# Linear attention, then a squared-ReLU MLP: q of the first batch in two halves, KV copy on VectorE, weight and v loads reordered, block sums later

## The chip, the cores and the metric

One core of one Trainium2 chip. The metric is the device time of one execution in microseconds (us). A time below is a median of the stated number of executions. The experiments ran on three chips (12, 13 and 14 in the record); each ratio is taken against executions of before from the same rounds.

## The reference

```python
# q, k, v: (8 batches, 8 heads, 576 tokens, 64); phi(x) = [relu(x)*cos, relu(x)*sin] by position
q_p, k_p = phi(q), phi(k)
kv  = einsum('bhsf,bhsd->bhfd', k_p, v);  z = sum_s(k_p)
x   = einsum('bhsf,bhfd->bhsd', q_p, kv) / (einsum('bhsf,bhf->bhs', q_p, z) + 1e-6)
h   = x.reshape(4608, 512) @ w_in          # w_in 512 x 2048
out = (relu(h)**2) @ w_out                 # w_out 2048 x 512
```

## The kernel before

Each batch has 512 tokens as four tiles of 128 and a tail of 64. TensorE works through a fixed list of "slots": for batch 0, slots 0 to 7 are eight steps of the hidden layer (`gemm1`) and 8 to 15 the output layer (`gemm2`); batch 1 has slots 16 to 25 and 26 to 33. Steps 0 to 3 take tiles 0 and 1 through the four blocks of w_in (512 columns each), steps 4 to 7 tiles 2 and 3. Pieces of the next batches' attention hang on slots. The order on every engine is the order of the program. From batch 1 on, part of the output layer uses sums and differences of w_out's blocks (`w2_sum`), so that fewer products are needed.

```python
def load(src, nm, b, eng):                       # q, k or v of one batch
    main = inp.tile([P, H, J, D], F32, name=nm, tag=nm, bufs=2)
    tail = inp.tile([P, HH, D], F32, name=nm + "t", tag=nm + "t", bufs=2)
    eng.dma_start(out=main[:, :, :, :],
                  in_=src[b, :, 0:MAIN, :].rearrange("h (p j) d -> p h j d", j=J))
    ...                                          # two DMAs for the tail

def att_kv(b, part):
    ...                                          # KV and z of all heads, in PSUM
    if part == 1:
        nc.scalar.copy(out=kvzs[b].rearrange("p (a h) e -> p a (h e)", a=2),
                       in_=kz[:, :, 0 : HH * E1])

def gemm1(b, s):
    ...
    step = P if b == 0 and s % 4 == 0 else w     # 128 columns at a time, or 256
    for c in range(0, w, step):
        for i in range(nh):
            for kb in range(KB):
                nc.tensor.matmul(out=hps[:, i, c:c+step], lhsT=w1sb[:, kb, hb*P:(hb+1)*P], ...)
    nc.scalar.activation(out=rt, in_=hps, func=ACTF.Relu)   # the square, on VectorE, follows

# the start
load_batch(0, nc.sync, "kvq")
constants(); warm(34)                            # matmuls of zeros
...                                              # features of k, casts of v
att_v(0, J - 1, nc.gpsimd, H - 1, H)             # a small GpSimd cast: it waits for v,
for i in range(4): load_w1(i, 4)                 # and so w_in's loads start behind v
load_batch(1, nc.gpsimd, "q")
load_w2(0, 4)
load_batch(1, nc.gpsimd, "kv")
for i in range(1, 4): load_w2(i, 4)
load_batch(2, nc.gpsimd, "qkv")
att_kv(0, 0); att_kv(0, 1)
warm(8)
att_feat(0, 0); att_feat(0, 1)
...                                              # transposes, numerator, division, transposes
for s in range(len(slots)): run(s)
```

## Time and profile before

| what | before |
|---|---|
| time | 290.11 us, median of 3 (289.47 to 290.32) |
| span in the profile | 288.9 us, and that execution took 290.67 us |
| TensorE busy, clock granted | 97%, 1.00 |
| first hidden-layer matmul | 19.18 us |
| GpSimd's DMA queue idle before q's tail of batch 2 | 11.34 us, to 47.53 us |
| first numerator of batch 2 | 79.32 us, with a wait |

The span is the time from the first to the last instruction in the profile; the time adds some 1.8 us. But for a few short holes before 100 us, TensorE is full from the first hidden-layer matmul to its last one, which ends at 285.5 us. The change leaves the last 3.4 us, without matmuls, as they are, so a microsecond is won only before 19 us or in a hole (a stretch in which TensorE waits).

### The profile page before, as it was taken

What the parts mean: (1) busy time and instruction counts of PE and PEld (TensorE: products, weight loads), DVE (VectorE), ACT (ScalarE), POOL (GpSimd) and SP (SyncE); (2) the same over time, 40 slices, a digit from 0 to 9 for tenths busy, and PEclk for the clock granted to TensorE, in tenths of its full rate; (3) what the DMA queues carried; (4) which work ended last, traced back from release to release, by engine and by line L of the source; (5) the groups of instructions that cost most, each with busy time, mean ns of one, the idle gap of its engine ahead of it and who ended that gap; (6) DMA issues with size and microseconds to landing.
All of it is one profiled execution on the core that took longest, in us unless ns stands there. A gap on an engine that the chain in (4) does not pass through costs nothing.

```text
span 288.9 us, 7286 instructions
## 1 busy us (share of the span) xinstructions
PE 281.2 (97%) x3038; PEld 236.0 (82%) x3045; DVE 202.0 (70%) x452; ACT 163.8 (57%) x249; POOL 39.1 (14%) x67
## 2 busy tenths in 40 slices
PE   8989999999899999999999999999999999999995
PEld 3569855788568888898988888888998988889884
DVE  1367765597399399877598777977677877547485
ACT  3476653579758759555783358835695551155210
POOL 1462604660000000100002000000000000000002
PEclk9999999999999999999999999999999999999999
DMA  7999995999988899899519985399808530200015
GB/s 209 298 203 283 355 210 182 317 355 278 121 150 199 151 295 208 207 284 255 167 75 205 336 181 166 93 248 310 220 16 204 144 49 2 122 26 0 2 73 148
DMA packets 76785, 53.04 MB, mean 184 GB/s; under 512 B 52016, under 2 KB 71984, under 8 KB 76752
## 3 DMA queue, kind: packets, MB, share of 16 engines
q1 hardware_dynamic: 66960, 29.24, 46.4%
q0 software_dynamic: 9648, 23.20, 27.6%
q8 instruction: 24, 0.39, 0.6%
q10 hardware_dynamic: 144, 0.13, 0.1%
q14 instruction: 9, 0.07, 0.1%
HBM read 36.70 MB, written 9.44 MB: 160 GB/s over the span
## 4 chain that ended last, share of the span: by engine, by line
PE 84%; DMA 8%; DVE 3%; SPq 2%; ACT 1%; issue 1%; ACTq 0%
PE hps L383 40%; PE ya L525 9%; PE yc L525 9%; PE yu L525 7%; DMA qpT<-qp 5%; PE yv L525 5%; PE num L310 3%; DMA q<-in_q_dram 3%; PE yps L432 2%; PE kz L241 2%; PE yh L432 2%; PE tq L284 1%; SPq L69 1%; PE yps L456 1%; DVE ysb L537 1%
## 5 line engine op out<-in xcount | busy, mean ns | idle before, releaser
L383 PEld LDWEIGHTS <-w1sb 128*128 128x128 bf16 x1312 | 112.9, 98 | 12.7 <-issue 2.0
L383 PE MATMUL hps<-xT,w1sb 128*128 128x256 bf16 (+1 forms) x1056 | 119.1, 269 | 0.7 <-ACT rt L391 0.2
L391 ACT ACTIVATE rt<-hps 128x1024 bf16<-128x1024 f32 x72 | 73.7, 1024 | 66.1 <-PE hps L383 43.7
L398 DVE TENSOR_TENSOR gT<-rt 128x1024 bf16<-128x1024 bf16 x64 | 43.9, 686 | 20.9 <-ACT rt L391 20.9
L525 PEld LDWEIGHTS <-gs 128*128 128x128 bf16 x480 | 46.8, 98 | 5.4
L525 PEld LDWEIGHTS <-gT 128*128 128x128 bf16 x312 | 29.8, 98 | 3.5
L410 POOL DMA_DIRECT2D out_dram<-ysb x14 | 7.6, 542 | 170.8 <-DVE ysb L537 144.9
L181 ACT ACTIVATE kp<-k,sin_col 128x512 bf16<-128x512 f32 x32 | 22.4, 717 | 3.0 <-DMA k<-in_k_dram 3.0
L324 DVE TENSOR_TENSOR x<-num,rden 128x512 bf16<-128x512 f32 x32 | 22.1, 691 | 1.1
L181 ACT ACTIVATE qp<-q,sin_col 128x512 bf16<-128x512 f32 x32 | 22.1, 722 | 0.8 <-DMA q<-in_q_dram 0.7
L320 DVE TENSOR_SCALAR den<-num 128x8 f32<-128x8 f32 (+1 forms) x40 | 6.5, 163 | 21.7 <-PE num L310 21.6
L521 DVE TENSOR_TENSOR gs<-gT 128x1024 bf16<-128x1024 bf16 x26 | 17.8, 684 | 0.0
L171 DVE TENSOR_SCALAR qp<-q,cos_col 128x512 bf16<-128x512 f32 x32 | 15.1, 497 | 1.7 <-DMA q<-in_q_dram 1.7
L525 PE MATMUL ya<-w2t,gs 128*128 128x256 bf16 x120 | 15.6, 273 | 0.0
L525 PE MATMUL yc<-w2sb,gs 128*128 128x256 bf16 x120 | 15.6, 273 | 0.0
L525 PE MATMUL yu<-w2t,gs 128*128 128x256 bf16 x120 | 15.6, 273 | 0.0
L383 PE MATMUL hps<-xTt,w1sb 128*128 128x128 bf16 x256 | 15.1, 219 | 0.2 <-ACT rt L391 0.2
L200 ACT CAST vext<-v 128x512 bf16<-128x512 f32 x23 | 14.1, 614 | 1.8 <-DMA v<-in_v_dram 1.8
L525 PE MATMUL yu<-w2sb,gs 128*128 128x256 bf16 x112 | 14.5, 273 | 0.0
L576 ACT COPY s<-yu 128x256 f32<-128x256 f32 x14 | 5.2, 373 | 15.6 <-PE yu L525 15.6
L525 PE MATMUL yc<-w2sb,gT 128*128 128x256 bf16 x104 | 13.5, 273 | 0.0
L525 PE MATMUL yv<-w2t,gT 128*128 128x256 bf16 x104 | 13.5, 273 | 0.0
(97 smaller groups left out, 333.5 us busy)
## 6 DMA issues: line engine op xcount, KB each, us to landing
out_dram<-ysb POOLq DMA_DIRECT2D x14, 512.0 KB, 4.5
k<-in_k_dram SPq DMA_DIRECT2D x5, 1024.0 KB, 7.5
v<-in_v_dram SPq DMA_DIRECT2D x5, 1024.0 KB, 8.2
q<-in_q_dram SPq DMA_DIRECT2D x5, 1024.0 KB, 6.1
q<-in_q_dram POOLq DMA_DIRECT2D x3, 1024.0 KB, 12.5
k<-in_k_dram POOLq DMA_DIRECT2D x3, 1024.0 KB, 9.0
v<-in_v_dram POOLq DMA_DIRECT2D x3, 1024.0 KB, 8.9
w1sb<-in_moe_w_in_dram POOLq DMA_DIRECT2D x4, 512.0 KB, 8.7
```

Of the source, the lines that this page charges most:

```text
L171: nc.vector.tensor_scalar(out=dst[:, :, 0:D], in0=src, scalar1=0.0, scalar2=cos_col[:, j : j + 1], op0=ALU.max, op1=ALU.mult,)
L181: nc.scalar.activation(out=dst[:, :, D:F], in_=src, func=ACTF.Relu, scale=sin_col[:, j : j + 1])
L200: copy(out=vx[:, j, h0:h1, 0:D], in_=piece("v", b, j)[:, h0:h1, :])
L310: nc.tensor.matmul(out=out, lhsT=lhsT, rhs=kvz[:, half * HH + hh, :], start=True, stop=True)
L324: nc.vector.tensor_tensor(out=x_of(b, j).rearrange("p (b k) (l d) -> p b k l d", b=n, l=2), in0=n4[:, :, :, 0:D].rearrange("p b (k l) d -> ...
L383: nc.tensor.matmul(out=out, lhsT=w1sb[:, kb, hb * P : (hb + 1) * P], rhs=rhs, start=(kb == 0), stop=(kb == KB - 1),)
L391: nc.scalar.activation(out=rt[:, :, :], in_=hps[:, :, :], func=ACTF.Relu)
L398: nc.vector.tensor_tensor(out=dst, in0=rt[:, :, :], in1=rt[:, :, :], op=ALU.mult)
L410: eng.dma_start(out=dst, in_=y.rearrange("p i c -> p (i c)") if n > 1 else y[:, c0:c1])
L432: nc.tensor.matmul(out=ypss[b][tt], lhsT=gTs[b][:, hb, tt * P : (tt + 1) * P], rhs=w2sb[:, hb, :], start=(hb == 0), stop=(hb == HB - 1),)
L521: nc.vector.tensor_tensor(out=t[:, :, :], in0=in0, in1=in1, op=op)
L525: nc.tensor.matmul(out=acc, lhsT=lhs[:, hb, :], rhs=rhs[:, hb, :], start=(hb == 0), stop=(hb == HB2 - 1),)
```

## The change

Intent: let the first two tiles of batch 0 start when half of q has landed; keep the KV copy out of ScalarE's way; let w_out's second block arrive before TensorE needs it; shift batch 1's attention by a slot as its v then lands later; take the block sums off VectorE where it was full.

```diff
-    def load(src, nm, b, eng):
+    def load(src, nm, b, eng, parts=1):
...
+        for i in range(parts):
+            js = slice(i * J // parts, (i + 1) * J // parts)
+            eng.dma_start(
+                out=main[:, :, js, :],
+                in_=src[b, :, 0:MAIN, :].rearrange("h (p j) d -> p h j d", j=J)[:, :, js, :],
+            )
...
-        if part == 1:
-            nc.scalar.copy(...)
+        if part == 1 and b:
+            att_kvz(b, nc.scalar.copy)
+
+    def att_kvz(b, copy):
+        copy(out=kvzs[b]..., in_=kzs[b][:, :, 0 : HH * E1])
...
-        step = P if b == 0 and s % 4 == 0 else w
+        step = P if b < 2 and s in (0, 4) else w
...
-    at(18, att_d, 0, J)
-    at(19, att_x_pe, 0, J, True)
+    at(19, att_d, 0, J)
+    at(20, att_x_pe, 0, J, True)
     plan(
         1,
         k=(8, 8, 8, 9, 9),
         f=(4, 5, 6, 12, 13),
-        kv=(10, 10),
-        d=(11, 13, 15, 17, 19),
-        t=(5, 6, 7, 16, 17),
-        x=(12, 14, 16, 18, 20),
+        v=(10, 10, 10, 10, 10),
+        kv=(11, 11),
+        d=(12, 14, 16, 17, 20),
+        t=(5, 6, 7, 16, 19),
+        x=(13, 15, 17, 18, 21),       # and the odd tiles' and the tail's copies go to VectorE
...
-    for n, s in ((1, 12), (2, 15)):
-        at(s, w2_sum, n)
-    for n, s, c in ((4, 18, 0), (4, 19, 1), (3, 30, 0), (3, 31, 1)):
-        late.setdefault(s, []).append((w2_sum, (n, c * HB2 // 2, (c + 1) * HB2 // 2)))
+    at(13, w2_sum, 1)
+    for n, s in ((2, 22), (4, 24), (3, 30)):
+        for c in range(2): ...        # half in slot s, half in s + 1
...
-        load_batch(0, nc.sync, "kvq")
+        load_batch(0, nc.sync, "kv")
+        load(q, "q", 0, nc.sync, 2)
...
-        load_batch(1, nc.gpsimd, "kv")
-        for i in range(1, 4):
+        load_batch(1, nc.gpsimd, "k")
+        load_w2(1, 4)
+        load_batch(1, nc.gpsimd, "v")
+        for i in range(2, 4):
             load_w2(i, 4)
...
-        warm(8)
         att_feat(0, 0)
         att_feat(0, 1)
+        att_kvz(0, nc.vector.tensor_copy)
+        warm(1)
```

More of the change, by code (lines that the diff above doesn't have):

```diff
@@ L59 @@
     kqv = {}
-    def load(src, nm, b, eng):
+    def load(src, nm, b, eng, parts=1):
         main = inp.tile([P, H, J, D], F32, name=nm, tag=nm, bufs=2)
         tail = inp.tile([P, HH, D], F32, name=nm + "t", tag=nm + "t", bufs=2)
-        eng.dma_start(
-            out=main[:, :, :, :],
-            in_=src[b, :, 0:MAIN, :].rearrange("h (p j) d -> p h j d", j=J),
-        )
+        for i in range(parts):
[4 more added lines that the diff above has]
+            )
         for g in range(2):
@@ L247, in att_kv @@
                     )
-        if part == 1:
-            nc.scalar.copy(
-                out=kvzs[b].rearrange("p (a h) e -> p a (h e)", a=2),
-                in_=kz[:, :, 0 : HH * E1],
-            )
+        if part == 1 and b:
+            att_kvz(b, nc.scalar.copy)
+    def att_kvz(b, copy):
+        copy(
+            out=kvzs[b].rearrange("p (a h) e -> p a (h e)", a=2),
+            in_=kzs[b][:, :, 0 : HH * E1],
+        )
     def att_feat(b, j, parts="cs"):
@@ L635, in att_t, with plan @@
         att_qT_copy(b, j)
-    def plan(b, k, f, kv, d, t=(), x=(), act_cos=(1, 3), act_v=range(NS)):
+    def plan(b, k, f, kv, d, t=(), x=(), act_cos=(1, 3), act_v=range(NS), v=None):
         for j in range(NS):
@@ L642, in plan @@
             at(k[j], att_k, b, j, feat_cos_act if j in act_cos else feat_cos)
-            at(k[j], att_v, b, j, nc.scalar if j in act_v else nc.vector)
+            at((v or k)[j], att_v, b, j, nc.scalar if j in act_v else nc.vector)
             at(f[j], att_feat, b, j)
-            if t:
+            if j < len(t):
                 at(t[j], att_t, b, j)
@@ L649, in plan @@
             at(d[j], att_d, b, j)
-            if x:
-                at(x[j], att_x_pe, b, j, x[j] > 16)
+            if j < len(x):
+                at(x[j], att_x_pe, b, j, x[j] > 16, nc.vector.tensor_copy if last else nc.scalar.copy)
             elif last:
@@ L711 @@
     late = {}
-    for n, s in ((1, 12), (2, 15)):
-        at(s, w2_sum, n)
-    for n, s, c in ((4, 18, 0), (4, 19, 1), (3, 30, 0), (3, 31, 1)):
-        late.setdefault(s, []).append((w2_sum, (n, c * HB2 // 2, (c + 1) * HB2 // 2)))
+    at(13, w2_sum, 1)
+    for n, s in ((2, 22), (4, 24), (3, 30)):
+        for c in range(2):
+            chunk = (n, c * HB2 // 2, (c + 1) * HB2 // 2)
+            late.setdefault(s + c, []).append((w2_sum, chunk))
     for b in range(1, B):
```

## The prediction

> **What bounds the kernel now.** I read the page first (busy shares, slices), then the chain of waits up to 112 us, then the time line around the start, then the landings of the weight loads, then the list of waits.
>
> ```profile
> PE 281.2 (97%) x3038; PEld 236.0 (82%) x3045; DVE 202.0 (70%) x452; ACT 163.8 (57%) x249; POOL 39.1 (14%) x67
> PEclk9999999999999999999999999999999999999999
> ...
> 0.00:19.20 19.20, 17.00 (x128) 8.36 (x131) 8.16 (x26) 10.13 (x17) 8.67 (x19) 1.00 0.95 241
> 19.20:36.50 17.30, 17.30 (x226) 15.99 (x224) 11.27 (x26) 10.74 (x14) 6.74 (x9) 1.00 1.13 300
> 36.50:53.20 16.70, 16.23 (x136) 8.59 (x137) 9.06 (x23) 7.31 (x13) 5.67 (x9) 1.00 0.88 206
> 53.20:79.30 26.10, 25.08 (x305) 20.99 (x303) 18.73 (x42) 20.87 (x32) 7.39 (x11) 1.00 1.13 268
> ```
>
> The kernel is bound by TensorE in program order: 97% busy, full clock throughout. The stretches (length, then busy time of TensorE, weight load, VectorE, ScalarE, GpSimd) show it packed from 19.2 us on; most of the 17.0 us before that are warming matmuls with no use. So only two things can be won: the 19 us before the first hidden-layer matmul, and about 1.5 us of small holes before 100 us. From 100 us on the change alters nothing.
>
> ```profile
> 5.58 8.55 DMA q<-in_q_dram
> 14.13 0.02 issue
> 14.15 0.73 ACT qp L181
> ...
> 16.29 0.42 PE num L310 x8
> ...
> 18.95 0.40 PE tx L351 x4
> 19.35 1.79 PE hps L383 x32
> ...
> 64.33 14.94 DMA qpT<-qp
> 79.27 0.05 issue
> 79.32 0.42 PE num L310 x8
> ```
>
> This is the chain of waits (start, length, what). The start hangs on q of batch 0, landing at 14.13 us: features, transposes, numerator at 16.29, division, transposes, first hidden-layer matmul at about 19.2. Later the chain passes once through a transfer: the transposed q of batch 2, issued at 64.33, landing at 79.27.
>
> ```profile
> 19.98 0.64 POOL L69 DMA_DIRECT2D kt<-in_k_dram  x1 [1.33 <-DMA w1sb<-in_moe_w_in_dram]
> 23.42 0.62 POOL L69 DMA_DIRECT2D kt<-in_k_dram  x1 [2.80 <-DMA w1sb<-in_moe_w_in_dram]
> 25.93 0.90 POOL L64 DMA_DIRECT2D v<-in_v_dram  x1 [1.89 <-DMA w1sb<-in_moe_w_in_dram]
> ...
> 21.86 1.91 PE L383 MATMUL hps<-xT,w1sb 128*128 128x256 bf16 x16
> 23.85 1.91 PE L383 MATMUL hps<-xT,w1sb 128*128 128x256 bf16 x16
> 26.07 1.91 PE L383 MATMUL hps<-xT,w1sb 128*128 128x256 bf16 x16
> 71.91 1.95 PE L383 MATMUL hps<-xTt,w1sb 128*128 128x128 bf16 x32 [0.23 <-ACT rt L391]
> ```
>
> This is the time line. GpSimd's queue is released by landings of w_in's blocks; the semaphore records give the landings themselves: 17.11, 19.70, 23.14 and 25.65 us. TensorE uses blocks 1, 2 and 3 at 21.86, 23.85 and 26.07. So block 2 has 0.71 us in hand and block 3 only 0.42. That is the central fact of this prediction: q is the first wall, w_in stands close behind it.
>
> **What the Trainium skill says.** "DMA: Bandwidth & Descriptors", section "Why small descriptors are slow (HBM only)": every packet carries a fixed overhead beside its bytes. The trace agrees: in the q, k and v loads of the start a 1024-byte packet took 46 ns and a 256-byte packet (the tails) 18 ns, so about 8.7 ns fixed and 0.0365 ns a byte. The same page, "Issuing engines are not separate DMA queues": transfers from all queues share the same 16 engines. The trace agrees: with w_in alone in flight the stream wrote some 195 KB/us (bf16, so twice that read), and the weights then queue in order. "VectorE: DVE Perf Modes", "Why PSUM operands drop a tier": an fp32 source in PSUM goes at the slow rate. The trace's nearest case is x from PSUM: 0.69 us for 128x512, against 0.42 us for a v cast of that size from SBUF. "TensorE: Matmul & The Clock Gate", "Why this matters for your kernels": idle gaps over some 3 us halve the clock. Gaps here stay under 1 us with the clock at 1.00, so I hold dropping 7 of 8 warming matmuls for safe.
>
> **The change, part by part.**
>
> q in halves. A half has runs of 512 bytes instead of 1024. Estimate for a packet: 8.7 + 512 x 0.0365 = 27.4 ns. Each engine moves 64 packets of 1024 bytes now: 64 x 46 = 2.94 us. The first half is 64 packets of 27.4 ns = 1.75 us. So it lands 1.19 us earlier, at about 12.94; the second half lands 0.56 us later than q does now, at about 14.7, ahead of its need (features of tiles 2 and 3, 16.68 now).
>
> KV copy on VectorE. From 12.94: the two cosine features take 1.10 us, to 14.07; then the copy, about 0.65 by the x row, to 14.72; then the copy of the first transposes, 0.45, to 15.2. On ScalarE the two sine features (1.34) end at 14.3 and its copy (0.59) by 14.9. So the numerator starts at about 15.25 instead of 16.29: of 1.19 us, 1.04 remain, as VectorE now carries the KV copy in that chain. ScalarE would have done it before the features in a quiet time; the reason for the move is that KV (done at 12.83) now comes at the same moment as q. Fewer warming matmuls only keep TensorE free. First hidden-layer matmul: about 18.1 instead of 19.18.
>
> What w_in leaves of it. TensorE would reach block 2 at 23.85 - 1.05 = 22.8, but it lands at 23.14; it would reach block 3 at 25.3 or so, but that lands at 25.65, or about 0.1 later as q's 0.56 us of extra packet time lies partly beside block 0. So hidden-layer step 3 starts at about 25.8 instead of 26.07. Of 1.04 us, 0.27 remain. w_in's issue does not move: it follows v (10.97) at 11.45.
>
> w_out block 2 ahead of v. It landed at 40.15; hidden units 8 and 9 need it 16 matmuls after 36.56 plus holes, near 40.4. Without the swap a start 0.27 us earlier would just touch that. With the swap it lands near 37; v takes its place near 40.2, and its casts (5 of 0.42 or less, to 42.3) precede the KV product, now a slot later near 44. So this saves nothing by itself, it avoids a new wait.
>
> Slots of batch 1 and the earlier loads. The tail of q of batch 2 is held until batch 0's tail features are done: VectorE ran them at 46.64, behind a division; the load was issued at 47.53 after an 11.34 us wait. Now they precede that division, and ScalarE's sine (after the KV copy, a slot later) ends near 46.1. So the queue restarts about 0.9 us earlier, and the loads of batches 2 and 3 with it.
>
> Two hidden-layer steps of batch 1 in halves: in each, 32 matmuls of 128 columns (1.79 us, as in batch 0's first step) take the place of 16 of 256 (1.75 us): +0.04 each, +0.08. It lets the step begin before the second tile's transpose has been copied.
>
> Block sums and copies. VectorE loses 1.21 + 2 x 0.68 us between 54 and 66 us and gets 4 x 0.68 later, behind the squares of slots 22 to 25. Before the next squares it idles 0.97, 0.83, 0.88 and then 3.23 us now, so each sum fits. ScalarE gives three copies of x transposes (0.58, 0.58, 0.37) to VectorE; it runs without a break from 64.6 to 76 us and caused the 0.23 us hole at 71.91, which should close: -0.23.
>
> The q transpose of batch 2. TensorE would reach it at 78.67 - 0.27 - 0.23 + 0.08 = 78.25. Its transfer, slowed by the loads of batch 3 and the stores of batch 0, should land up to 0.9 us before 79.27, say at 78.45. So TensorE passes at about 78.5 instead of 79.32. The gain of the whole is that: about 0.8 us, of which 0.27 come from the start, 0.23 from ScalarE, the rest from that shorter wait, less 0.08. 290.1 - 0.8 = 289.3.
>
> **The rivals.** (a) All of the start survives: if w_in's blocks landed a microsecond earlier, the first 1.04 us would be kept, with the other parts 1.6 to 1.8 us: 288.4. Against it: the w_in stream is saturated and its issue unmoved. (b) The gain is swallowed by transfers: q's small packets delay block 3 by the full 0.56 us, to 26.2, and the q transpose lands as late as now; then everything meets again at 79.3 and the time stays at 290.1. For it: the transpose took 14.94 us against a median of 4.2, so contention decides it. (c) VectorE becomes late around 67 to 76 us: the added sums use 2.7 us of the 3.2 us idle there; if one delays the KV product of batch 2, up to 0.6 us are lost: 289.9. (d) The clock drops at the start with 7 fewer warming matmuls: some 3 us at half rate, 1 to 1.5 us lost: 290.8. The clock row speaks against it.
>
> **Range and chances.** (a) I give 20%, (b) 25%, (c) and (d) together 15%, the sum 40%. Predicted 289.3 us; the runs before spread over 0.85 us (289.47 to 290.32), so 288.3 to 290.3 should hold it 8 times in 10. 2% are 5.8 us, more than the whole removable idle time after 19 us and the start's gain together; faster 1%, within 2% 98%, slower 1%.
>
> **What would show it.** Landing of the first q half near 12.9 (packets of 512 bytes near 27 ns); numerator near 15.25; first hidden-layer matmul near 18.1; then new waits of TensorE for w_in before steps 2 and 3, the latter near 25.8; the wait at 71.91 gone; the restart of GpSimd's queue near 46.6; the numerator of batch 2 near 78.5; and from there the same distances to the end. It is wrong if step 3 starts before 25.3 (w_in no wall), if the clock row falls below 9, or if the numerator of batch 2 does not come earlier than 79.

## The result, and the profile after

289.75 us, median of 4 (289.61 to 290.22), against 289.81 us for 4 executions of before (289.47 to 290.32). The ratio is 0.9999, with a 95% interval of 0.9978 to 1.0021: the same. Ratios are the mean time of one kernel's fast runs over that of the other's of the same rounds, so not quite the ratio of the medians quoted. The predicted 289.3 us is 0.45 us below, inside the noise of the comparison; the predicted gain of 0.8 us did not show in the times. The predicted range, 288.3 to 290.3, also held the 290.1 of no gain at all, so that the time lies in it says little.

The profile tells more. The page's first row and the table of stretches (start:end, length, busy time of TensorE, weight load, VectorE, ScalarE, GpSimd), cut at the events that ended the stretches before:

```profile
PE 280.6 (97%) x3070; PEld 236.0 (82%) x3070; DVE 204.5 (71%) x457; ACT 161.8 (56%) x245; POOL 39.0 (14%) x67
...
0.00:18.00 18.00, 15.58 (x123) 7.84 (x124) 8.47 (x27) 9.58 (x16) 7.88 (x19) 1.00 0.93 239
18.00:36.60 18.60, 17.89 (x227) 16.05 (x225) 12.17 (x26) 10.81 (x14) 7.25 (x10) 1.00 1.17 282
36.60:53.05 16.45, 16.25 (x132) 8.32 (x130) 9.12 (x24) 6.66 (x12) 6.55 (x11) 1.00 0.90 245
53.05:78.60 25.55, 25.32 (x345) 21.73 (x342) 19.95 (x46) 19.56 (x29) 6.63 (x10) 1.00 1.06 279
```

The first stretch is 1.2 us shorter than before's, the second 1.3 us longer (18.60 against 17.30), with 0.71 us in which TensorE does nothing where it had been full. What the start won is gone 18 us later. The last stretch is 0.55 us shorter and nearly full. Now the chain of waits of after (start, length, what):

```profile
2.67 8.44 DMA v<-in_v_dram
11.65 2.56 POOL w1sb L119 x3
14.22 11.82 DMA w1sb<-in_moe_w_in_dram
26.09 1.92 PE hps L388 x16
```

Before, the start of this chain was q. Now it is v, then the issue of w_in behind v, then w_in's landing, then step 3. Neither q nor anything made from it is on it. TensorE's time line shows the waits:

```profile
15.09 0.40 PE L315 MATMUL num<-kvz,qpTp 128*128 128x65 bf16 x8
...
17.98 1.95 PE L388 MATMUL hps<-xT,w1sb 128*128 128x128 bf16 x32
...
21.02 1.92 PE L388 MATMUL hps<-xT,w1sb 128*128 128x256 bf16 x16 [0.20 <-DMA w1sb<-in_moe_w_in_dram]
...
23.55 1.92 PE L388 MATMUL hps<-xT,w1sb 128*128 128x256 bf16 x16 [0.36 <-DMA w1sb<-in_moe_w_in_dram]
...
26.09 1.92 PE L388 MATMUL hps<-xT,w1sb 128*128 128x256 bf16 x16
...
72.05 1.95 PE L388 MATMUL hps<-xTt,w1sb 128*128 128x128 bf16 x32 [0.23 <-ACT rt L396]
...
78.60 0.41 PE L315 MATMUL num<-kvz,qpT 128*128 128x65 bf16 x8
```

The numerator comes 1.20 us earlier than before, the first hidden-layer matmul 1.20 us, step 1 0.84, step 2 0.30, and step 3 0.02 us later. By the semaphore records w_in's blocks landed at 17.43, 20.98, 23.50 and 26.04 us. (A wait after the last matmul's modelled end shorter than 0.15 us has no bracket, so step 3's shows none; counted from matmul start to matmul start, beyond the usual pitch, the three waits are 0.36, 0.53 and 0.32 us.) Near 79 us the wait for batch 2's transposed q is gone, and the hole at 72 us stands as it stood.

**A clock for comparing profiles.** The landing of v of batch 0 moves from execution to execution: the first v cast of ScalarE (the conversion of v to bf16, which starts when v has landed) lies between 9.67 and 11.31 us over the 14 profiles. GpSimd issues w_in behind v's landing too, so that moves all that follows. Profiles are compared below from that cast on. Before's is at 10.99 us, after's at 11.13.

| run (profiled execution) | first hidden matmul | step 3 starts | span ends | hole at w_out block 1 | hole at batch 2's q |
|---|---|---|---|---|---|
| before | 8.20 | 15.08 | 277.91 | - | 0.65 |
| before_again | 8.21 | 15.09 | 278.04 | 0.84 | - |
| before_one_block | 8.20 | 15.09 | 277.03 | - | - |
| start_only | 6.73 | 14.71 | 277.49 | - | 0.65 |
| rest_only | 8.40 | 15.28 | 277.43 | - | - |
| after | 6.85 | 14.96 | 276.97 | - | - |
| after_again | 6.72 | 14.92 | 276.88 | - | - |
| after_one_block | 6.72 | 13.60 | 275.55 | - | - |
| qt_later | 7.43 | 15.19 | 277.31 | - | - |
| w1_early | 6.72 | 14.65 | 276.60 | - | - |
| w1_split | 6.72 | 14.33 | 276.28 | - | - |
| w1_split_qt | 6.72 | 14.36 | 276.47 | - | - |
| v_on_dve | 6.74 | 14.71 | 276.50 | - | - |
| best | 7.36 | 14.60 | 276.38 | - | - |

All in us after ScalarE's first v cast; the holes as TensorE's idle time. (The two of 0.65 carry 0.70 in the time line of their profile, counted from a modelled matmul end; 0.65 is counted from starts.)

### The profile page after: what moved, and what is told of

Read it like the earlier page. It is cut to its first block, busy times and chain, and to the rows that moved or that the text cites. A ratio compares the mean times of both kernels' runs of the same rounds, so it can differ in the third digit from the quotient of the medians.

```text
span 288.1 us, 7340 instructions
## 1 busy us (share of the span) xinstructions
PE 280.6 (97%) x3070; PEld 236.0 (82%) x3070; DVE 204.5 (71%) x457; ACT 161.8 (56%) x245; POOL 39.0 (14%) x67
## 4 chain that ended last, share of the span: by engine, by line
PE 85%; DMA 7%; DVE 2%; ACT 2%; issue 1%; POOL 1%; SPq 1%; ACTq 0%
PE hps L388 40%; PE ya L530 9%; PE yc L530 9%; PE yu L530 7%; PE yv L530 5%; DMA w1sb<-in_moe_w_in_dram 4%; PE num L315 3%; DMA v<-in_v_dram 3%; PE kz L243 3%; PE yps L461 2%; PE yps L437 2%; PE yh L437 2%; DVE ysb L542 1%; POOL w1sb L119 1%; PE tq L289 1%
## 5 line engine op out<-in xcount | busy, mean ns | idle before, releaser
L173 DVE TENSOR_SCALAR qp<-q,cos_col 128x512 bf16<-128x512 f32 x32 | 15.9, 524 | 0.4 <-DMA q<-in_q_dram 0.4
L530 PE MATMUL yu<-w2sb,gs 128*128 128x256 bf16 x112 | 14.5, 273 | 0.0
```

The source lines that it names most:

```text
L173: nc.vector.tensor_scalar(out=dst[:, :, 0:D], in0=src, scalar1=0.0, scalar2=cos_col[:, j : j + 1], op0=ALU.max, op1=ALU.mult,)
L530: nc.tensor.matmul(out=acc, lhsT=lhs[:, hb, :], rhs=rhs[:, hb, :], start=(hb == 0), stop=(hb == HB2 - 1),)
```

## The experiments

The theory: w_in's landing, which follows v and not q, is the wall; what the start wins is lost there; the rest of the change removes waits that before has in some executions. Rivals: something else holds the chain; the rest of the change loses what the start wins; the first profile of before misled.

**before_again and after_again: both kernels unchanged, for more times and a second profile of each.**

> The kernel before, unchanged, to see how much one profile of it says. Theory 1 (the profile of before that the prediction rests on caught a late landing of batch 2's transposed q; typical runs land earlier): the span is 288.0 to 288.4 us instead of 288.9, and the wait of TensorE at the first numerator of batch 2, 0.65 us in that profile, is under 0.3 us here. Theory 2 (the wait belongs to this kernel and the change removes it): wait again 0.5 to 0.8 us and span near 288.9. Ratio 1.000 in both.

> The changed kernel, unchanged, for a second profile and more times. Theory 1 (the change is worth nothing at the end, because w_in's landing gives back the start): waits of 0.3 to 0.5 us before steps 1, 2 and 3 again; time within 0.3 us of before, ratio 0.999 to 1.001. Theory 2 (the first profile, 0.97 us shorter than before when counted from the landing of v, is typical and the four times were an unlucky draw): ratio 0.996 to 0.998. In both no wait at w_out block 1 nor at batch 2's transposed q.

before_again: 290.29 us (6 runs), ratio 1.0011 (0.9996 to 1.0025); its profile's span is 288.7 us. after_again: 289.28 us (6 runs), ratio 0.9987 (0.9968 to 1.0005), span 287.9 us. Neither theory on before_again held: the wait for batch 2's q was absent, yet the span was as long. Another wait stood in its place, seen in TensorE's time line of before_again:

```profile
41.04 0.59 PE L432 MATMUL yh<-w2sb,gT 128*128 128x512 bf16 x2 [0.84 <-DMA w2sb<-in_moe_w_out_dram]
```

TensorE waits for w_out's second block. In the first profile that block had landed in time, and the prediction took that for the rule. So before has two places where a load is late in some executions and in time in others. After and after_again have neither, and waits for w_in are there in both (0.32, 0.33 and 0.17 us of idle time in after_again). The ratio of after_again leaves the gain open between 0.3% and nothing. Together, the 10 executions of after have a mean of 289.47 us; the 52 fast ones of before, taken beside all runs, 289.90. These are not all of the same rounds; at most this says some 0.4 us, or 0.15%.

**start_only: the start of after in before.** Halves of q, KV copy on VectorE, one warming matmul; all else as before.

```diff
 # before, with
+        load_batch(0, nc.sync, "kv"); load(q, "q", 0, nc.sync, 2)
+        att_kvz(0, nc.vector.tensor_copy); warm(1)      # behind the two att_feat
```

> Before, with only the start changed: q of batch 0 in halves, KV copy on VectorE, one warming matmul. Theory (w_in's landing is the wall): first hidden-layer matmul near 18.0 us as in after, waits for w_in before steps 1, 2 and 3, step 3 again at 25.8 to 26.2, time within 0.2 us of before (ratio 0.9993 to 1.0007). Rival (the start is worth what it saves, and the rest of the change loses it again): ratio 0.996, step 3 near 25.

290.55 us (6 runs), ratio 1.0029 (1.0005 to 1.0052). The first hidden-layer matmul is 6.73 us behind the v cast, as in after; step 3 at 14.71, against 15.08 in before: of 1.47 us, 0.37 were left. (By the span's own clock step 3 is at 24.81 us, ahead of the expected 25.8 to 26.2, as v landed early, at 10.10.) The wait for the transposed q is there:

```profile
78.09 0.42 PE L315 MATMUL num<-kvz,qpT 128*128 128x65 bf16 x8 [0.70 <-DMA qpT<-qp]
```

The theory expected no gain and got none. That the six times are longer and more spread than before's (289.47 to 291.99) it did not expect; the profiled execution is one of the short ones (289.51), so the cause stays open. The rival's 0.996 is excluded.

**rest_only: after with the start of before.**

```diff
 # after, with
-        load_batch(0, nc.sync, "kv"); load(q, "q", 0, nc.sync, 2)
+        load_batch(0, nc.sync, "kvq")
 # and the KV copy on ScalarE, warm(8) ahead of the features
```

> After, with the start of before (q whole, KV copy on ScalarE, eight warming matmuls): only the order of loads, the slots of batch 1 and the later block sums. Theory: first hidden-layer matmul at 19.2, no waits for w_in, step 3 at 26.1 as in before; the loads of batches 2 and 3 some 0.5 to 0.9 us earlier than in before; time within 0.3 us of before (ratio 0.999 to 1.001). Rival (this part wins 0.5 us or more through an earlier q transpose of batch 2): ratio 0.998 or below.

289.86 us (6 runs), ratio 0.9995 (0.998 to 1.001): within what the theory allowed. Its profile has neither of before's two waits. From step 3 to the end it takes 262.15 us, as after does (262.01) and as before_one_block, a profile of before's order with both loads in time, does (261.94); before takes 262.83 and before_again 262.95. So from there on it is 0.7 to 0.9 us shorter than where before is late, and no shorter than where before is not. How much of this the change does and how much is chance comes below.

**after_one_block and before_one_block: w_in's wall taken away.** Steps 0 to 3 of batch 0 all use w_in's first block. Their outputs are wrong, which doesn't matter for the times. The matmuls are the same in number and shape.

```diff
                 hb = h0 + i
+                hw = i if b == 0 and s < 4 else hb
...
-                        lhsT=w1sb[:, kb, hb * P : (hb + 1) * P],
+                        lhsT=w1sb[:, kb, hw * P : (hw + 1) * P],
```

> After, with steps 0 to 3 of batch 0's hidden layer all using w_in's first block (wrong result for half of batch 0's tokens, on purpose; the same matmuls, no wait for blocks 1 to 3). Theory (w_in's landing is the wall): steps 1 to 3 without waits, step 3 at 24.9 to 25.1 instead of 26.09; of the 1.1 us some is given back at the next walls (q of batch 1 at 28.9, the qpT copies at 37.6), so the time falls by 0.5 to 1.1 us, ratio 0.996 to 0.998. Rival (something else holds the chain, w_in is only what is met first): ratio 0.9993 or above, the time given back before 40 us.

> Before, with steps 0 to 3 of batch 0's hidden layer all on w_in's first block (wrong result on purpose). Control for the same edit on after, which won 1.55 us. Theory (before reaches steps 2 and 3 just behind the landings, so it has no such wall): ratio 0.998 to 1.001, step 3 at the same 14.5 us after the first KV matmul. Rival (the edit wins by itself, through weights that stay the same): ratio 0.995 as on after.

On after: 288.32 us (5 runs), ratio 0.9945 (0.9933 to 0.9957). On before: 290.08 us (6 runs), ratio 1.0037 (1.0006 to 1.0068). TensorE's time line of after_one_block:

```profile
17.71 1.95 PE L389 MATMUL hps<-xT,w1sb 128*128 128x128 bf16 x32
...
20.39 1.91 PE L389 MATMUL hps<-xT,w1sb 128*128 128x256 bf16 x16
...
22.38 1.91 PE L389 MATMUL hps<-xT,w1sb 128*128 128x256 bf16 x16
...
24.59 1.91 PE L389 MATMUL hps<-xT,w1sb 128*128 128x256 bf16 x16
```

No wait is left, step 3 comes at 13.60 us behind the v cast instead of 14.96, and the span ends at 275.55 instead of 276.97. The 1.36 us at step 3 arrive whole at the end: no wall further on takes them back, which I had expected in part. On before the same edit moves step 3 by 0.01 us on the scale from v; steps 2 and 3 of before_one_block:

```profile
24.01 1.91 PE L384 MATMUL hps<-xT,w1sb 128*128 128x256 bf16 x16
...
26.22 1.91 PE L384 MATMUL hps<-xT,w1sb 128*128 128x256 bf16 x16
```

So it is not the edit that wins but the wait, and only a kernel with the early start meets the wait. This shows the cause: the start of after is worth about 1.4 us, and w_in's landing keeps most of it, all but 0.1 to 0.4 us (step 3 at 14.92 and 14.96 in the profiles of after, at 14.71 in start_only and v_on_dve, which have the same start; 15.08 and 15.09 in before's). That before_one_block came out slower in the times rests on two long executions (291.75 and 292.31); its profile is the shortest of those with before's order.

**qt_later: q's tails behind the weights.**

```diff
-        load(q, "q", 0, nc.sync, 2)
+        load(q, "q", 0, nc.sync, 2, False)        # no tails here
...
         load_w2(0, 4)
+        load_tails(q, "q", 0, nc.gpsimd)
```

> After, with the two tail loads of q of batch 0 (0.58 us of 256-byte packets an engine) moved from ahead of w_in to behind w_out's first block. Theory (w_in's landing sets the time): w_in's last block lands 0.2 to 0.6 us earlier counted from the first KV matmul (14.43 in after), step 3 as much earlier, time down by that, ratio 0.998 to 0.9995. Rival (the loads' time is set by w_in's own stream from its issue on, whatever lies before): landing as in after, ratio 0.9995 to 1.0005.

289.42 us (6 runs), ratio 0.9992 (0.997 to 1.0014). Inconclusive: in this profile v landed unusually early (cast at 9.67 us), TensorE's warming matmuls still ran, and the scale from v does not fit. Against w_in's issue, its last block landed 14.69 us later, in after 14.45: the tails did not hold it up visibly.

**w1_early: w_in's first block issued ahead of v's landing.** A small GpSimd copy of finished k features takes the place of the wait for v.

```diff
+        gate = att.tile([P, HH, F], BF16, name="gate")
+        nc.gpsimd.tensor_copy(out=gate[:, :, :], in_=kp_of(0, J))
+        nc.gpsimd.tensor_copy(out=gate[:, 0:2, :], in_=kp_of(0, J)[:, 0:2, :])
+        load_w1(0, 4)
         att_v(0, J - 1, nc.gpsimd, H - 1, H)
...
-        for i in range(4):
+        for i in range(1, 4):
             load_w1(i, 4)
```

> After, with w_in's first block issued after two GpSimd copies of a finished k feature (estimated 10.6 to 11.0 us) instead of after v's landing (11.59). Theory (w_in's landing sets the time, and its stream starts when it is issued): blocks land 0.4 to 0.9 us earlier, step 3 at 25.2 to 25.7 on the scale where it was 26.09, ratio 0.997 to 0.9985; q's second half lands later but is not needed before 15.5. Rival (bandwidth is full then, so what w_in wins q's halves lose): first numerator 0.3 us or more later than 15.09, time as after or worse, ratio 0.9995 to 1.002.

289.81 us (6 runs), ratio 1.0001 (0.9974 to 1.0028). Issued at 10.24 us, with v cast at 10.48; blocks landed at 16.88, 20.04, 22.54 and 25.08 us, step 3 at 25.13. From the v cast that is 14.65 instead of 14.94, so 0.3 us of the 0.4 to 0.9 expected, and only 0.06 us ahead of the 14.71 that start_only and v_on_dve reach without this edit: a gain is not shown. The first data moved 2.12 us behind the issue, in after 1.65. The times do not tell it from after.

**w1_split and w1_split_qt: w_in's last block in two halves**, alone and with q's tails moved.

```diff
-        for i in range(4):
+        for i in range(3):
             load_w1(i, 4)
+        for i in range(6, 8):
+            load_w1(i, 8)
```

> After, with w_in's last block (512 columns) loaded as two of 256. Theory (TensorE waits for a whole block, and the last block's landing sets step 3 and with it the end): the first half lands about 1.2 us before the second; step 3's first 8 matmuls start at 25.3 to 25.6 on the scale where it was 26.09, its last 8 at 26.2 to 26.5[...]; step 3 ends 0.4 to 0.7 us earlier and so does the kernel: ratio against before 0.9965 to 0.998, and 0.4 to 0.7 us under after's 289.3 to 289.75. Rival (a wall further on, q of batch 1 or the qpT copies at 37.6, gives that back): step 3 earlier, but the first output matmul of batch 0 no earlier than 15.6 us after step 0's start plus what after had (25.0 from the first KV matmul).

> After, with both the split of w_in's last block and q's tails behind w_out's first block. Theory: the gains add where the landing still binds: waits before steps 1 and 2 shrink by 0.2 to 0.4 us against the split alone, ratio against before 0.995 to 0.9975. Rival (q's tails cost nothing, as w_in's stream is set by its issue): same as the split alone within 0.2 us.

w1_split: 288.99 us (6 runs), ratio 0.9967 (0.9938 to 0.9997). w1_split_qt: 289.03 us (6 runs), ratio 0.9967 (0.9935 to 0.9998). TensorE's time line of w1_split:

```profile
20.33 1.92 PE L388 MATMUL hps<-xT,w1sb 128*128 128x256 bf16 x16
...
22.83 1.92 PE L388 MATMUL hps<-xT,w1sb 128*128 128x256 bf16 x16 [0.33 <-DMA w1sb<-in_moe_w_in_dram]
...
25.05 1.91 PE L388 MATMUL hps<-xT,w1sb 128*128 128x256 bf16 x16
```

Step 3 now starts where TensorE gets to it: the first half landed at 24.11 us, the second at 25.52, ahead of the ninth matmul. It starts at 14.33 us behind the v cast, 0.61 us before after's mean of 14.94 and 0.38 before the earliest of the four profiles with this start and a whole last block (14.71). From step 3 to the end it takes as long as after (261.95 us, in after 262.01 and 261.96), so the gain of 0.4 to 0.6 us arrives at the end. The smaller packets had a price: from block 2's landing to the whole of block 3's it took 2.74 us, in after 2.54. Moving q's tails added nothing (14.36), which with qt_later answers for the rival there.

**v_on_dve: why the hole at 72 us did not close.** One v cast of batch 2 on VectorE, the sums two slots later.

```diff
-        act_v=(1, 3),
+        act_v=(3,),
...
-    for n, s in ((2, 22), (4, 24), (3, 30)):
+    for n, s in ((2, 24), (4, 26), (3, 30)):
```

> After, with the v cast of batch 2's second tile on VectorE instead of ScalarE, and the later block sums of w_out two slots later still to make room. It tests why the hole near 72 us (0.39 us over the matmul pitch, the same in six profiles) did not close. Theory (it is local: three ScalarE pieces, 2.04 us, stand between two evictions of 1.75 us pitch, whatever backlog there was before): one piece of 0.61 us less closes it to under 0.15 us, ratio against after 0.999, against before 0.997 to 0.9995. Rival (the eviction waits for VectorE's squares, so VectorE's extra cast makes it worse): hole as large or larger, a later start of batch 2's KV product.

289.07 us (6 runs), ratio 0.9973 (0.9945 to 1.0002). ScalarE's time line of after, then of v_on_dve:

```profile
68.33 1.02 ACT L396 ACTIVATE rt<-hps 128x1024 bf16<-128x1024 f32 x1 [0.23 <-PE hps L388]
69.25 0.71 ACT L183 ACTIVATE kp<-k,sin_col 128x512 bf16<-128x512 f32 x1
69.86 0.61 ACT L202 CAST vext<-v 128x512 bf16<-128x512 f32 x1
70.37 0.72 ACT L183 ACTIVATE qp<-q,sin_col 128x512 bf16<-128x512 f32 x1
70.99 1.01 ACT L396 ACTIVATE rt<-hps 128x1024 bf16<-128x1024 f32 x1
```

```profile
67.68 1.02 ACT L396 ACTIVATE rt<-hps 128x1024 bf16<-128x1024 f32 x1 [0.22 <-PE hps L388]
68.60 0.71 ACT L183 ACTIVATE kp<-k,sin_col 128x512 bf16<-128x512 f32 x1
69.22 0.71 ACT L183 ACTIVATE qp<-q,sin_col 128x512 bf16<-128x512 f32 x1
69.83 1.01 ACT L396 ACTIVATE rt<-hps 128x1024 bf16<-128x1024 f32 x1
```

In after ScalarE idles for 0.23 us just ahead, so it has no backlog; then three pieces stand between two evictions (ScalarE's `rt<-hps`, which reads a step's sums so that TensorE can reuse their place), which are 2.66 us apart while TensorE makes one step in 1.75. With one piece less they are 2.15 us apart and TensorE's hole is gone. But it is partly given back: near 105 us the numerator of batch 3, 0.13 us late in after, is 0.34 us late here, as VectorE's division comes later. From the start of step 3's last matmul to the end it is 260.14 us, against 260.34 in after (mean of two): 0.2 us won of the 0.39.

**best: split, early issue and v cast together.**

> After with the three edits together that shortened the profile counted from ScalarE's first v cast: w_in's last block in two halves (276.28 against 276.9), its first block issued ahead of v's landing (276.60), and the v cast on VectorE with later sums (276.50). Theory (w_in's landing first, then local holes): they add nearly, end at 275.4 to 275.9 on that scale; time 288.0 to 288.6, ratio against before 0.993 to 0.9965. Rival (the three share one slack, and a wall further on takes what is above the best of them): end at 276.2 or later, ratio 0.9965 to 0.998.

289.24 us (6 runs), ratio 0.9985 (0.9957 to 1.0013): missed; the span ends at 276.38 us, no better than the split alone. TensorE's time line:

```profile
18.61 1.96 PE L388 MATMUL hps<-xT,w1sb 128*128 128x128 bf16 x32
...
23.63 1.92 PE L388 MATMUL hps<-xT,w1sb 128*128 128x256 bf16 x16 [0.17 <-DMA w1sb<-in_moe_w_in_dram]
```

The first step itself starts at 7.36 us behind the v cast instead of 6.72: the numerator was already 0.34 us late (4.17 instead of 3.83 in after_again), as VectorE did the KV copy later, and 0.29 us are a wait for w_in. w_in's first block, issued at 10.62, landed at 18.57, later than the 17.43 of after, where it was issued at 11.59; q's tails landed at 16.59 and 18.41, in after at 14.69 and 14.93. So both the early weights and the rest of q landed late; that they were in each other's way is likely, not shown. The issue came 0.63 us ahead of the v cast, in w1_early only 0.24 ahead, and there the same edit did the first step no harm (first block at 16.88; the tails at 13.95 and 16.50). So the early issue is a gamble, and w1_split, with an interval against before that lies below 1, is the version to keep: 288.99 us. How far it lies below after in time is not settled, as they were not run in the same rounds; the span from v says 0.64 us against after's two profiles.

## Why the prediction was right or wrong

**q's half, right.** Packets of 512 bytes took 27 ns; the first half landed at 12.99 us (predicted 12.94), the second at 14.45 (14.7).

**The start's chain, right.** Numerator at 15.09 (15.25), first hidden-layer matmul at 17.98 (18.1). The KV copy took 0.69 us on VectorE (0.65) and did lie between the features and the copy of the transposes. The clock stayed at 1.00; rival (d) fell.

**What w_in leaves of it, right.** The prediction let 0.27 us through. From the v cast, step 3 moved from 15.09 to 14.94 in after's two profiles, so 0.15 us; in start_only and v_on_dve to 14.71, so 0.37 us. The mean of the four is 0.26 us. The term is the last block's landing, predicted 0.1 us later than before. It was at 14.66 and 14.70 us behind the v cast in before, at 14.91 and 14.87 in after, but at 14.66 in both start_only and v_on_dve: that the halves of q delay it is not shown. That w_in is the wall is shown by after_one_block. One wait was not foreseen, the 0.36 us before step 1: block 1 landed at 20.98 us, in the profile that the prediction used at 19.70. In before_one_block, with before's order, it landed at 21.33, so this too varies from one execution to the next. (The stream's rate was read a little low: from 14.5 to 23 us of before, with w_in all but alone, GpSimd's queue wrote 202 KB/us, not 195.)

**w_out's second block, wrong.** "This saves nothing by itself" was read from one profile, in which the block arrived 0.25 us before its use. In before_again it landed at 41.00 us and cost 0.84 us of idle time. With the swap it landed at 36.5 to 37.8 us in all ten profiles, and TensorE needs it near 40, so this wait is removed by the change.

**The queue's restart, right.** GpSimd's queue issued the held tail at 46.60 us (46.6); this is its line in after:

```profile
46.60 1.25 POOL L71 DMA_DIRECT2D qt<-in_q_dram  x2 [9.90 <-ACT qpt L183]
```

**The hole at 72 us, wrong.** The step that failed is "which should close: -0.23". It took a busy stretch of ScalarE for a backlog, so that less work anywhere before would help. It has the same 0.39 us beyond the pitch in the twelve profiles with the old cast, whatever came before. It is the work between two evictions that counts, and v_on_dve, which cut that, closed it.

**The transposed q of batch 2, right at the numerator (78.60, predicted 78.5), wrong in how.** Its transfer landed at 76.31 us in after, 3.0 us earlier than in the profile of before, not 0.9; the wait is not shortened but gone. But that is not shown to be the change's doing. The prediction took a transfer of 14.94 us (issue to landing) as before's own, and in before_again the unchanged kernel's took 9.13:

```profile
L267 SPq DMA_TRANSPOSE qpT<-qp x1: 6849/6849/6849, 64.9 to 64.9; - x1
...
DMA to landing us min/median/max: 9.1/9.1/9.1
```

It landed at 74.08 us, ahead of its need even without w_out's wait. Over the four profiles with before's order of loads it took 9.1, 9.8, 14.9 and 14.9 us, over the ten with after's 10.4 to 12.5: the order may keep the long ones away, but two of four are too few to say.

**The sum.** The spans of the two profiles differ by 0.8 us (288.9 and 288.1), just as predicted, but by luck; the times do not. The prediction took the profile of before as a picture of its typical execution. But that one had a 0.65 us wait that before_again and before_one_block do not have, and 290.67 us against a median of 289.8. Against before_one_block, before's order with both loads in time, after ends 0.06 us earlier, with step 3 0.13 us earlier. (The 0.08 us estimated for the two steps of 128 columns does not show: after_again and after_one_block, which have them, take 261.96 and 261.94 us from step 3 to the end, before_one_block 261.94.) So of the predicted 0.8 us this went missing: the 0.23 us of the hole at 72 us, which stayed, and the 0.4 us of the shorter wait for q, which only some executions of before have. The start's 0.27 us came through, as 0.15 to 0.37; the rest of its 1.2 to 1.5 us stayed at w_in's wall, as predicted. The swap of the loads takes away a late w_out block, which cost before_again 0.84 us and before nothing. Rival (b), to which I gave 25%, has the nearest time, but not the mechanism: in after q's transpose did not land late.

What stays open: why start_only's times are longer and wider than before's, and how often before is late. Three of four profiles with before's order of loads have one of the two waits, none of ten with after's; but the times of the executions that were not profiled do not tell their waits. For w_out's block the reordering is the cause; for the transposed q that is open.

## What to carry to other kernels

Before shortening a start, ask what TensorE will need next and when it lands: a transfer that was hidden by 0.4 us becomes the wall as soon as the first one moves by more. When a wall is a load, split it so that work can begin on its first half; here that carried 0.4 to 0.6 us to the end where the whole earlier change, in two profiles, had carried about 0.1. Take two or three profiles of the kernel before, and time them from a common event, before reading tenths of a microsecond from one.

## What the Trainium skill lacked or had wrong

- "DMA: Bandwidth & Descriptors", "Specifications": it gives about 1 us to the first byte for loads issued from GpSimd. Here w_in's first data moved 1.62 us (before) and 1.65 us (after) behind the start of the issuing instruction, and 2.12 us in w1_early, with q still in flight.
- The same page, "Latency and other measured facts": it says that two of the DMA engines are usually slower, and ascribes it, as a best guess, to loads issued from GpSimd alone. Here, of the 16 shares of one v load issued from SyncE, fourteen landed from 8.96 to 10.31 us and the last two at 11.07 and 11.11 (after), before any load was issued from GpSimd (at 11.59 us; its data moved from 13.2 us on). The trace does not say which engines these were, so this is a doubt and not a refutation.
- The same page, "Why small descriptors are slow (HBM only)": it works out 256-byte packets in cycles. The runs add packet times on the SyncE queue: 18, 27 and 46 ns for 256, 512 and 1024 bytes; and, for w_in's cast packets on GpSimd's queue, 98 ns for 1024 bytes written and 60 ns for 512 (w1_split).
- No page tells how long a DMA transpose takes beside other traffic: one that lands within 4.2 us (median in before) took 9.1 to 14.9 us over the 14 profiles beside the loads of batch 3 and the first stores.
- No page says how much the landing of one and the same load moves between executions: 1.6 us here (v cast at 9.67 to 11.31 us).
